# Linear attention and two feed-forward blocks on one core: VectorE's order written out for sixteen slots, the weight decode cut in other pieces

## The chip, the core and the metric

The kernel runs on one core of a Trainium2 chip. The metric is the device time of one execution in microseconds (us), the median of three runs. The engines are TensorE (PE: matmuls; PEld is its weight load), VectorE (DVE), ScalarE (ACT), GpSimd (POOL) and SyncE (SP, whose queue issues the transfers). They run side by side, each through its own list of instructions in order, and wait for each other through semaphores.

## The reference

Three stages follow each other. The first is a linear attention with a decaying state (batch 4, 8 heads, 768 steps, 48 wide), here as the recurrence that defines it:

```
cur   = (u * k_t) v_t^T
y_t   = r_t (state + cur)
state = w_t * state + k_t v_t^T
```

The second is a feed-forward block on the 3072 tokens that come out, 384 wide, with 2048 inner columns:

```
h = x @ w_in ;  g = h * clip(h + 3, 0, 6) / 6 ;  x = g @ w_out
```

The third is like it with 1024 inner columns, a softmax gate and a layer norm between its two products. The weights of both blocks come as float64, so their words have to be turned into float32 on the chip.

## The kernel before, in words

The attention works on tiles of 128 steps. One batch entry has six tiles, and tile number i is step block i // 4 of batch entry i % 4, so the state of a batch entry is needed again four tiles on. 512 tokens (four tiles) make a group of the first feed-forward block. A group takes 16 **slots**, one for each chunk of 128 inner columns; there are six groups and so 96 slots. Slot n issues `ffn_in(n)` (9 matmuls into h, L715, then ScalarE's t at L719, VectorE's gate at L720 and ScalarE's rounded copy gh at L721; GpSimd makes the rest gl at L729), then pieces of the attention of a later tile, then `ffn_out(n-2)` (9 matmuls, L740). Products are made three times, high by high, high by low and low by high part, so each operand has a high (`..h`) and a low (`..l`) half. The buffers `h` are two, so `ffn_in(n)` needs the gate of slot n-2 to be done.

In slots 0 to 15 a second stream runs along: the 16 chunks of the weights (`w1`) are decoded, chunk m needed by slot m. Chunks 0 to 2 are made ahead of the slots. Slot n then finishes chunk n+3 (`w1_b`), begins chunk n+4 (`w1_a`) and issues the load of chunk n+6 (`w1_load`, four transfers into one of three `raw` buffers). One chunk has 128x768 words in pairs, low word and high word of a float64:

- L63, ScalarE: absolute value of the high word times a power of two, into `dec`.
- L66, VectorE: the sign bit of the high word, in place in `raw`. It has to come after L63, which reads the same words.
- L50, VectorE: `dec` shifted left by 3, with the sign. L53, VectorE: the top 3 bits of the low word added. After L53 the `raw` buffer is free.
- L71, ScalarE: `w1_h`, the rounded copy. L72, VectorE: `w1_l`, what is left over.

The attention of tile 4+n//4 is spread over four slots; j is n % 4. Its VectorE work: in slot j=0 the masks' copies (L625, two of them, whose other operand ScalarE makes at L620); two state adds (L644), which need the products kv of TensorE (L635); in slot j=2 the output's low half xl (L686; its high half xh is ScalarE's L685). For the next tile then the scans over the decay, q (L525, four) and e (L529, L531 four, L535), and the product with the keys (L549), on which TensorE's transposes ktp (L578) wait. TensorE's small products share three buffers (`ps_a`) in turn, so rt (L489) waits until the state adds have read kv, and kt (L489) until xl has read yt.

What sets the order: through the whole loop only SP's list stands as written. The lists of the other engines come from the scheduler of the framework, which moved VectorE's instructions among the slots: the pieces of the decode of three chunks lie between those of the attention.

Of the kernel before, what the change touches and what calls it, by code (L numbers as in the profile page):

```python
# [8 lines left out]
F32 = mybir.dt.float32  # L9
BF16 = mybir.dt.bfloat16  # L10
F32R = mybir.dt.float32r
I32 = mybir.dt.int32
ACTF = mybir.ActivationFunctionType
ALU = mybir.AluOpType
# [4 lines left out]
P = 128  # L19
W_LO, W_HI = 0.75, 1.25  # L20
SIGN = -(2**31)
# [26 lines left out]
def dec_b(nc, raw, f):  # L48

    nc.vector.scalar_tensor_tensor(  # L50
        out=f, in0=f, scalar=3, in1=raw[:, :, 1], op0=ALU.logical_shift_left, op1=ALU.bitwise_or
    )
    nc.vector.scalar_tensor_tensor(  # L53
        out=f, in0=raw[:, :, 0], scalar=29, in1=f, op0=ALU.logical_shift_right, op1=ALU.bitwise_or
    )
    return f.bitcast(F32)


def dec_s(nc, pool, raw, total, bufs=2):

    f = pool.tile([P, raw.shape[1]], I32, tag="dec", name="dec", bufs=bufs)
    hw = raw[:, :, 1]
    nc.scalar.activation(  # L63
        out=f.bitcast(F32), in_=hw.bitcast(F32), func=ACTF.Abs, scale=2.0**-112, accum_out=total
    )
    nc.vector.tensor_scalar(out=hw, in0=hw, scalar1=SIGN, scalar2=None, op0=ALU.bitwise_and)  # L66
    return f


def split(nc, src, hi, lo, eng):  # L70
    nc.scalar.activation(out=hi, in_=src, func=ACTF.Copy)  # L71
    eng.tensor_tensor(out=lo, in0=src, in1=hi.bitcast(F32), op=ALU.subtract)  # L72
# [206 lines left out]
def fast_path(  # L279
# [14 lines left out]
    nc = tc.nc  # L294
    B, H, S, D = r.shape
# [8 lines left out]
    M1 = F1 // P  # L304
    M2 = F2 // P
    GT = B * C
    NTILE = NG * B
    NSLOT = NG * M1
    LAG = 2
    LATE = 10  # L310
    JOIN = 10
# [43 lines left out]
    w1_h = w1p.tile([P, M1, WN], F32R, name="w1_h")  # L355
# [16 lines left out]
        wst[m] = [t]  # L372

    def w1_a(m):
        wst[m].append(dec_s(nc, dec, wst[m][0], chk[:, 3 * NTILE + m:3 * NTILE + m + 1]))

    def w1_b(m):
        split(nc, dec_b(nc, *wst.pop(m)), w1_h[:, m, :], w1_l[:, m, :], nc.vector)


    s_st = []
# [127 lines left out]
        )  # L509

    def st0(i):
        a = at[i]
        g = i // B
        if i < LATE:
            wt = ps_in(i, "wt", "y0")
            trans(wt, a["w"])
            rt = ps_in(i, "rt", "y1")
            trans(rt, a["r"])
        else:
            wt, rt = flip("w"), flip("r")  # L520
        q = atp.tile([P, HP, C + 1], F32, tag="q", name="q")
        e = atp.tile([P, HP, C], F32, tag="e", name="e")
        nc.gpsimd.memset(q[0:DP, :, C:C + 1], 1.0)
        for hp in range(HP):
            nc.vector.tensor_tensor_scan(  # L525
                out=q[0:DP, hp, 0:C][:, ::-1], data0=wt[0:DP, hp, :][:, ::-1], data1=ones[0:DP, :],
                initial=1.0, op0=ALU.mult, op1=ALU.mult,
            )
        nc.vector.reciprocal(out=e[0:DP, :, 0], in_=q[0:DP, :, 0])  # L529
        for hp in range(HP):  # L530
            nc.vector.tensor_tensor_scan(  # L531
                out=e[0:DP, hp, 1:C], data0=wt[0:DP, hp, 0:C - 1], data1=ones[0:DP, 0:C - 1],
                initial=e[0:DP, hp, 0:1], op0=ALU.mult, op1=ALU.mult,
            )
        nc.vector.tensor_tensor(out=e[0:DP], in0=rt[0:DP], in1=e[0:DP], op=ALU.mult)  # L535
        a.update(q=q, e=e)

    def st1(i):
        a = at[i]
# [40 lines left out]
        nc.scalar.activation(out=ktok, in_=ktp[:, :, 0:DP], func=ACTF.Copy)  # L580
        a["ktok"] = ktok

    def scores(i):
        a = at[i]
        kq = a["q"][:, :, 1:C + 1]
        rr = a["e"]
        a["am"] = []
        pas = [ps_tile("pa0"), ps_tile("pa1")] if i < JOIN else late["pa"]
        d = atp.tile([P, H], F32, tag="d", name="d")
        nc.vector.tensor_reduce(out=d, in_=a["z"], axis=AX.X, op=ALU.add)  # L590
        if i < JOIN:
            mask, diag = (x.unsqueeze(1).to_broadcast([P, HP, C]) for x in (causal, ident))
            for j in range(HP):
                for hh, pa in enumerate(pas):
                    o = 64 * hh
                    nc.tensor.matmul(
                        out=pa[:, j, :], lhsT=kq[o:o + D, j, :], rhs=rr[o:o + D, j, :], start=True, stop=True
                    )
        else:
            mask, diag = late["mask"], late["diag"]  # L600
            d0 = d
            d = late["v"].tile([P, H], F32, tag="dt", name="dt")
            nc.gpsimd.tensor_copy(out=d[:, 0:4], in_=d0[:, 0:4])
            for o, n, t0 in turned:
                nc.gpsimd.tensor_copy(out=d[o:o + n, 4:8], in_=d0[t0:t0 + n, 4:8])
            for j in (0, 2, 1, 3):
                for ks in (0, 64):
                    for hh, pa in enumerate(pas):
                        o, p = 64 * hh, ks if j < 2 else 64 - ks
                        nc.tensor.matmul(  # L610
                            out=pa[p:p + 64, j, ks:C], lhsT=kq[o:o + D, j, ks:ks + 64], rhs=rr[o:o + D, j, ks:C],
                            start=True, stop=True, skip_group_check=True,
                        )
        dv = d.rearrange("p (j hh) -> p hh j", hh=2)
        for hh, pa in enumerate(pas):
            am = atp.tile([P, 4, C], F32, tag="am", name="am")
            a["am"].append(am)
            if i < JOIN:
                for j in range(HP):
                    nc.scalar.activation(out=am[:, j, :], in_=ident, func=ACTF.Copy, scale=dv[:, hh, j:j + 1])  # L620
            else:
                nc.gpsimd.tensor_tensor(
                    out=am, in0=diag, in1=dv[:, hh, :].unsqueeze(2).to_broadcast([P, HP, C]), op=ALU.mult,
                )
            nc.vector.copy_predicated(am, mask, pa)  # L625

    def state_add(i):
        a = at[i]
# [62 lines left out]
            scores(i)  # L691

    def st3(i):
        state_add(i)
        if JOIN <= i + 1 < NTILE:
            scores(i + 1)
        out_x(i)

    stages = [stw, st0, st1, st2, st3]


    g_t = {}
# [126 lines left out]
    def load_to(n):  # L829
        while nxt[0] < min(n, LATE):  # L830
            load_in(nxt[0])
            load_v(nxt[0])
            nxt[0] += 1

    LD = 3
# [10 lines left out]
    nxt[0] = 3  # L846
    starts = [0, 2, 3, 4]
    decodes = {4: [0, 1], 6: [2], 8: [3]}
    NS = len(stages)
    for tick in range(starts[-1] + NS):  # L850
        for i in range(B):
            s = tick - starts[i]
# [13 lines left out]
    for i in range(B, NTILE):  # L866
        for s in range(NS):
            back = 2 if s == NS - 1 else s - 3 if i < JOIN else s - 5
            sched.setdefault(4 * (i - B) + back, []).append((i, s))
    for n in sorted(q for q in sched if q < 0):  # L870
        for i, s in sched[n]:
            stages[s](i)
            if s == 3:
                load_to(i + 3)
    order = ctx.enter_context(ExitStack())
    order.enter_context(tc.manual_schedule(engines={mybir.EngineType.SP}))
    for n in range(NSLOT + LAG):
        if n < NSLOT:
            ffn_in(n)
        if n == 4 * (JOIN - B) - 2:  # L880
# [158 lines left out]
```

## Time and profile before

| | us |
|---|---|
| median of 3 runs | 769.21 (768.65 to 769.26) |
| the profiled execution, whole | 768.09 |
| its span in the trace | 766.3 |
| TensorE busy | 733.2 (96%) |
| VectorE busy | 530.8 (69%) |
| ScalarE busy | 355.6 (46%) |
| GpSimd busy | 225.7 (29%) |

The shares are means over the program. The change lies in slots 0 to 15, which are 104 us of it: slot 0 begins at 45.7 us and slot 16 at 149.5. What they say there has to be read from views of those stretches: the table by stretches (busy time of each engine, granted clock of TensorE, share of the DMA engines), the groups of instructions of one engine within a window, and the timeline of an engine, in which each row has its start, its duration and, in brackets, how long the engine had been idle ahead of it and what ended that. Rows that follow each other without a dependency overlap a little in the timeline, because an instruction's end is drawn after the next one's start.

### The profile page before, as it was taken

To read this page: it belongs to the slowest core of one execution; us is meant where nothing else is said; L and a number is where in the kernel's file an instruction comes from. 1 tells how busy PE (TensorE), PEld (TensorE's weight loads), DVE (VectorE), ACT (ScalarE), POOL (GpSimd) and SP (SyncE) were. 2 spreads that over 40 slices of the span, in tenths; PEclk is the share of its full clock that TensorE was granted. 3 is DMA by queue.
4 is the path that set the end of the run, shared out by engine and by line. 5 is a ranking of instruction groups with operands and counts; after the bars stand their busy time and mean duration, and the time that the engine had idled before them with its cause. 6 is when DMAs were issued, how large, how long until landed. Compare 5 with 4: busy or idle time off the path is not lost. (4 is left out here: it accounts for less than half of the span.)

```text
span 766.3 us, 14116 instructions
## 1 busy us (share of the span) xinstructions
PE 733.2 (96%) x5308; PEld 619.4 (81%) x5308; DVE 530.8 (69%) x1008; ACT 355.6 (46%) x727; POOL 225.7 (29%) x357
## 2 busy tenths in 40 slices
PE   7688997999999999999999999999999999999996
PEld 5456775888888888888888888888899999999995
DVE  6978898768777777777798845877655555555551
ACT  4675665643444443433334335554544444444442
POOL 5225426522322222233333311224322222222200
PEclk9798899999999999999999999999999999999999
DMA  9795763624444454435334204432211111111001
GB/s 164 177 168 137 178 140 93 127 69 98 96 94 95 120 108 96 97 107 117 70 75 113 53 1 125 125 103 62 73 42 42 42 52 42 42 42 42 32 21 36
DMA packets 151406, 67.31 MB, mean 88 GB/s; under 512 B 101793, under 2 KB 145953, under 8 KB 151329
## 3 DMA queue, kind: packets, MB, share of 16 engines
q1 hardware_dynamic: 151328, 66.32, 36.3%
q8 instruction: 44, 0.72, 0.4%
q14 instruction: 34, 0.27, 0.1%
HBM read 56.33 MB, written 9.44 MB: 86 GB/s over the span
## 5 line engine op out<-in xcount | busy, mean ns | idle before, releaser
L740 PE MATMUL y<-gh,w_h 128*128 128x512 f32 x288 | 116.1, 403 | 0.0
L715 PE MATMUL h<-xh,w_h 128*128 128x512 f32 x288 | 113.3, 394 | 0.7 <-ACT xh L685 0.7
L715 PE MATMUL h<-xl,w_h 128*128 128x512 f32 x288 | 113.3, 393 | 0.0
L740 PE MATMUL y<-gl,w_h 128*128 128x512 f32 x288 | 113.1, 393 | 0.0
L740 PE MATMUL y<-gh,w_l 128*128 128x512 f32 x288 | 113.0, 392 | 0.0
L715 PE MATMUL h<-xh,w_l 128*128 128x512 f32 x288 | 112.8, 392 | 0.0
L719 ACT ACTIVATE t<-h,cols 128x512 f32<-128x512 f32 x96 | 65.4, 682 | 87.4 <-PE h L715 87.2
L721 ACT ACTIVATE gh<-t 128x512 fp32r<-128x512 f32 x96 | 60.4, 629 | 96.5 <-DVE t L720 96.5
L720 DVE SCALAR_TENSOR_TENSOR t<-t,h 128x512 f32<-128x512 f32 x96 | 65.1, 679 | 38.1 <-ACT t L719 38.0
L729 DVE TENSOR_TENSOR gl<-t,gh 128x512 fp32r<-128x512 f32 x80 | 66.9, 836 | 21.1 <-ACT gh L721 19.0
L78 DVE TENSOR_REDUCE nm<-h 128x1 f32<-128x1024 f32 x24 | 29.4, 1224 | 61.5 <-PE h L946 61.5
L973 PE MATMUL po<-w_oh,qh 128*128 128x384 f32 x192 | 67.2, 350 | 0.3 <-ACT qh L962 0.3
L560 POOL TENSOR_TENSOR sp<-s_st,q 112x384 f32<-112x384 f32 x20 | 18.6, 931 | 163.1 <-PE yt L657 139.9
L740 PEld LDWEIGHTS y<-gh,w_h 128*128 128x128 f32 x288 | 54.4, 189 | 13.8 <-issue 2.8
L973 PE MATMUL po<-w_oh,ql 128*128 128x384 f32 x192 | 64.8, 337 | 0.1
L973 PE MATMUL po<-w_ol,qh 128*128 128x384 f32 x192 | 64.8, 338 | 0.0
L715 PEld LDWEIGHTS h<-xh,w_h 128*128 128x128 f32 x288 | 54.6, 190 | 12.5 <-ACT xh L685 0.9
L715 PEld LDWEIGHTS h<-xh,w_l 128*128 128x128 f32 x288 | 54.7, 190 | 11.5
L715 PEld LDWEIGHTS h<-xl,w_h 128*128 128x128 f32 x288 | 54.7, 190 | 11.4
L740 PEld LDWEIGHTS y<-gh,w_l 128*128 128x128 f32 x288 | 54.4, 189 | 11.6
L740 PEld LDWEIGHTS y<-gl,w_h 128*128 128x128 f32 x288 | 54.6, 190 | 10.2
L962 ACT ACTIVATE qh<-pt 128x512 fp32r<-128x512 f32 x48 | 26.1, 596 | 78.4 <-PE pt L960 78.4
(129 smaller groups left out, 1497.3 us busy)
## 6 DMA issues: line engine op xcount, KB each, us to landing
raw<-in_moe_w_out_dram SPq DMA_DIRECT2D x24, 384.0 KB, 6.0
raw<-in_moe_w_in_dram SPq DMA_DIRECT2D x48, 128.0 KB
r<-in_r_dram SPq DMA_DIRECT2D x24, 192.0 KB, 3.1
k<-in_k_dram SPq DMA_DIRECT2D x24, 192.0 KB, 3.7
y1d<-ye SPq DMA_DIRECT2D x18, 256.0 KB, 2.3
y<-y1d SPq DMA_DIRECT2D x24, 192.0 KB, 2.8
out_dram<-os SPq DMA_DIRECT2D x24, 192.0 KB, 1.9
v<-in_v_dram SPq DMA_DIRECT2D x20, 192.0 KB, 4.5
```

The source lines that it names most:

```text
L78: nc.vector.tensor_reduce(out=nm, in_=h, axis=AX.X, op=ALU.max, negate=True)
L560: nc.gpsimd.tensor_tensor(out=sp[0:DP], in0=s_st[b][0:DP], in1=q[0:DP, :, 0:1].to_broadcast([DP, HP, 2 * D]), op=ALU.mult)
L715: nc.tensor.matmul(out=h, lhsT=a, rhs=b, start=(j == 0), stop=(j == len(ops) - 1))
L719: nc.scalar.activation(out=t, in_=h, func=ACTF.Relu, bias=three)
L720: nc.vector.scalar_tensor_tensor(out=t, in0=t, scalar=6.0, in1=h, op0=ALU.min, op1=ALU.mult)
L721: nc.scalar.activation(out=gh, in_=t, func=ACTF.Copy)
L729: eng.tensor_tensor(out=gl, in0=t, in1=gh.bitcast(F32), op=ALU.subtract)
L740: nc.tensor.matmul(out=y_ps[g][c], lhsT=a, rhs=b, start=(m == 0 and j == 0), stop=(m == M1 - 1 and j == 2))
L962: nc.scalar.activation(out=qh[:, ms, :], in_=pt, func=ACTF.Copy)
L973: nc.tensor.matmul(out=po, lhsT=x[:, m, :], rhs=y[:, m, :], start=(n == 0), stop=(n == 3 * M2 - 1))
```

## The change

Slots 0 to 15 get a loop of their own, and in it VectorE's list too stands as written. Three things are in it.

The decode is cut otherwise. `dec_p` has ScalarE's absolute value as before, then two instructions of VectorE that write the low word's place instead of the high word's: the low word shifted right by 29 (L77 of the new kernel), then the sign bit of the high word joined to it (L78). Neither needs ScalarE's result. `dec_q` is one instruction (L84): `dec` shifted left by 3, joined with that word. The high copy is L403 (was L71) and the low half L407 (was L72). Four instructions of VectorE a chunk it was and is.

The written order of a slot: the merge (L84, L403) ahead of or behind `ffn_in`, the low half (L407) behind `ffn_out`, then L74, L77 and L78 of the next chunk. The copies of the masks (L669) are a step of their own, and the scans of the next tile are two steps: q in slot j=2, e and the product with the keys in slot j=3.

The state adds (L688, was L644) with TensorE's products kv and GpSimd's part of tiles 4 to 9 move from slot j=2 to slot j=1.

The lists of ScalarE, TensorE and GpSimd are still made by the scheduler, and change with it. SP's list is the same instruction for instruction.

```diff
--- before.py
+++ after.py
@@ -65,6 +65,26 @@
     )
     nc.vector.tensor_scalar(out=hw, in0=hw, scalar1=SIGN, scalar2=None, op0=ALU.bitwise_and)
     return f
+
+
+def dec_p(nc, pool, raw, total):
+
+    f = pool.tile([P, raw.shape[1]], I32, tag="dec", name="dec", bufs=2)
+    lw, hw = raw[:, :, 0], raw[:, :, 1]
+    nc.scalar.activation(
+        out=f.bitcast(F32), in_=hw.bitcast(F32), func=ACTF.Abs, scale=2.0**-112, accum_out=total
+    )
+    nc.vector.tensor_scalar(out=lw, in0=lw, scalar1=29, scalar2=None, op0=ALU.logical_shift_right)
+    nc.vector.scalar_tensor_tensor(out=lw, in0=hw, scalar=SIGN, in1=lw, op0=ALU.bitwise_and, op1=ALU.bitwise_or)
+    return f
+
+
+def dec_q(nc, raw, f):
+
+    nc.vector.scalar_tensor_tensor(
+        out=f, in0=f, scalar=3, in1=raw[:, :, 0], op0=ALU.logical_shift_left, op1=ALU.bitwise_or
+    )
+    return f.bitcast(F32)
 
 
 def split(nc, src, hi, lo, eng):
@@ -372,10 +392,21 @@
         wst[m] = [t]
 
     def w1_a(m):
-        wst[m].append(dec_s(nc, dec, wst[m][0], chk[:, 3 * NTILE + m:3 * NTILE + m + 1]))
+        wst[m].append(dec_p(nc, dec, wst[m][0], chk[:, 3 * NTILE + m:3 * NTILE + m + 1]))
 
     def w1_b(m):
-        split(nc, dec_b(nc, *wst.pop(m)), w1_h[:, m, :], w1_l[:, m, :], nc.vector)
+        w1_merge(m)
+        w1_low(m)
+
+    def w1_merge(m):
+        f = dec_q(nc, *wst.pop(m))
+        nc.scalar.activation(out=w1_h[:, m, :], in_=f, func=ACTF.Copy)
+        wst[m] = f
+
+    def w1_low(m):
+        nc.vector.tensor_tensor(
+            out=w1_l[:, m, :], in0=wst.pop(m), in1=w1_h[:, m, :].bitcast(F32), op=ALU.subtract
+        )
 
 
     s_st = []
@@ -509,6 +540,10 @@
         )
 
     def st0(i):
+        st0_q(i)
+        st0_e(i)
+
+    def st0_q(i):
         a = at[i]
         g = i // B
         if i < LATE:
@@ -526,6 +561,11 @@
                 out=q[0:DP, hp, 0:C][:, ::-1], data0=wt[0:DP, hp, :][:, ::-1], data1=ones[0:DP, :],
                 initial=1.0, op0=ALU.mult, op1=ALU.mult,
             )
+        a.update(q=q, e=e, wt=wt, rt=rt)
+
+    def st0_e(i):
+        a = at[i]
+        q, e, wt, rt = a["q"], a["e"], a.pop("wt"), a.pop("rt")
         nc.vector.reciprocal(out=e[0:DP, :, 0], in_=q[0:DP, :, 0])
         for hp in range(HP):
             nc.vector.tensor_tensor_scan(
@@ -533,7 +573,6 @@
                 initial=e[0:DP, hp, 0:1], op0=ALU.mult, op1=ALU.mult,
             )
         nc.vector.tensor_tensor(out=e[0:DP], in0=rt[0:DP], in1=e[0:DP], op=ALU.mult)
-        a.update(q=q, e=e)
 
     def st1(i):
         a = at[i]
@@ -580,11 +619,11 @@
         nc.scalar.activation(out=ktok, in_=ktp[:, :, 0:DP], func=ACTF.Copy)
         a["ktok"] = ktok
 
-    def scores(i):
+    def scores(i, later=False):
         a = at[i]
         kq = a["q"][:, :, 1:C + 1]
         rr = a["e"]
-        a["am"] = []
+        a["am"], a["masks"] = [], []
         pas = [ps_tile("pa0"), ps_tile("pa1")] if i < JOIN else late["pa"]
         d = atp.tile([P, H], F32, tag="d", name="d")
         nc.vector.tensor_reduce(out=d, in_=a["z"], axis=AX.X, op=ALU.add)
@@ -622,7 +661,12 @@
                 nc.gpsimd.tensor_tensor(
                     out=am, in0=diag, in1=dv[:, hh, :].unsqueeze(2).to_broadcast([P, HP, C]), op=ALU.mult,
                 )
-            nc.vector.copy_predicated(am, mask, pa)
+            a["masks"].append((am, mask, pa))
+            if not later:
+                am_copy(i)
+
+    def am_copy(i):
+        nc.vector.copy_predicated(*at[i]["masks"].pop(0))
 
     def state_add(i):
         a = at[i]
@@ -691,12 +735,13 @@
             scores(i)
 
     def st3(i):
-        state_add(i)
+        if not B <= i < JOIN:
+            state_add(i)
         if JOIN <= i + 1 < NTILE:
             scores(i + 1)
         out_x(i)
 
-    stages = [stw, st0, st1, st2, st3]
+    stages = [stw, st0, st1, st2, st3, state_add]
 
 
     g_t = {}
@@ -846,7 +891,7 @@
     nxt[0] = 3
     starts = [0, 2, 3, 4]
     decodes = {4: [0, 1], 6: [2], 8: [3]}
-    NS = len(stages)
+    NS = len(stages) - 1
     for tick in range(starts[-1] + NS):
         for i in range(B):
             s = tick - starts[i]
@@ -867,14 +912,55 @@
         for s in range(NS):
             back = 2 if s == NS - 1 else s - 3 if i < JOIN else s - 5
             sched.setdefault(4 * (i - B) + back, []).append((i, s))
+        if i < JOIN:
+            sched.setdefault(4 * (i - B) + 1, []).append((i, NS))
     for n in sorted(q for q in sched if q < 0):
         for i, s in sched[n]:
             stages[s](i)
             if s == 3:
                 load_to(i + 3)
     order = ctx.enter_context(ExitStack())
+    order.enter_context(tc.manual_schedule(engines={mybir.EngineType.SP, mybir.EngineType.DVE}))
+    for n in range(M1):
+        j, ti = n % 4, B + n // 4
+        if j == 0:
+            w1_merge(n + LD) if n + LD < M1 else None
+            keys_in(ti)
+            scores(ti, later=True)
+            ffn_in(n)
+        elif j == 1:
+            am_copy(ti)
+            w1_merge(n + LD) if n + LD < M1 else None
+            state_add(ti)
+            ffn_in(n)
+            stw(ti + 1)
+        elif j == 2:
+            w1_merge(n + LD) if n + LD < M1 else None
+            ffn_in(n)
+            out_x(ti)
+        else:
+            st0_e(ti + 1)
+            ffn_in(n)
+            w1_merge(n + LD) if n + LD < M1 else None
+            st1(ti + 1)
+        if j == 0:
+            load_to(ti + 3)
+        if n >= LAG:
+            ffn_out(n - LAG)
+        if n + LD < M1:
+            w1_low(n + LD)
+        if n + LD + 1 < M1:
+            w1_a(n + LD + 1)
+        if n + LD + 3 < M1:
+            w1_load(n + LD + 3)
+        if j == 0:
+            am_copy(ti)
+        if j == 2:
+            st0_q(ti + 1)
+    order.close()
+    order = ctx.enter_context(ExitStack())
     order.enter_context(tc.manual_schedule(engines={mybir.EngineType.SP}))
-    for n in range(NSLOT + LAG):
+    for n in range(M1, NSLOT + LAG):
         if n < NSLOT:
             ffn_in(n)
         if n == 4 * (JOIN - B) - 2:
```

VectorE's list in slots 5 and 6, before (dec_1000, dec_1041 are the chunks 8 and 9, raw_1003 the words of chunk 10; t is the gate, xl the output's low half, q and e the scans of the next tile):

```order
L720 SCALAR_TENSOR_TENSOR t_1059<-t_1059,h_1049 128x512
L644 TENSOR_TENSOR s_st1_115<-kv_1066,sp_900 48x4x48
L72 TENSOR_TENSOR w1_l_112<-dec_1000,w1_h_111 128x768
L644 TENSOR_TENSOR s_st1_115<-kv_1066,sp_900 48x4x48
L686 TENSOR_TENSOR xl_828<-yt_1077,xh_827 128x3x128
L525 SCALAR_TENSOR_TENSOR q_1118<-wt_1108,ones_91 112x128 x4
L50 SCALAR_TENSOR_TENSOR dec_1041<-dec_1041,raw_923 128x768
L529 RECIPROCAL e_1119<-q_1118 112x4
L66 TENSOR_SCALAR raw_1003<-raw_1003 128x768
L531 SCALAR_TENSOR_TENSOR e_1119<-wt_1108,e_1119,ones_91 112x127 x4
L53 SCALAR_TENSOR_TENSOR dec_1041<-raw_923,dec_1041 128x768
L535 TENSOR_TENSOR e_1119<-rt_1113,e_1119 112x512
```

The same place in the new kernel (dec_1052 is chunk 9, raw_1002 the words of chunk 10):

```order
L688 TENSOR_TENSOR s_st1_115<-kv_1011,sp_903 48x4x48 x2
L765 SCALAR_TENSOR_TENSOR t_1032<-t_1032,h_1022 128x512
L407 TENSOR_TENSOR w1_l_112<-dec_998,w1_h_111 128x768
L77 TENSOR_SCALAR raw_924<-raw_924 128x768
L78 SCALAR_TENSOR_TENSOR raw_924<-raw_924 128x768
L84 SCALAR_TENSOR_TENSOR dec_1052<-dec_1052,raw_924 128x768
L765 SCALAR_TENSOR_TENSOR t_1073<-t_1073,h_1063 128x512
L730 TENSOR_TENSOR xl_831<-yt_1080,xh_830 128x3x128
L407 TENSOR_TENSOR w1_l_112<-dec_1052,w1_h_111 128x768
L77 TENSOR_SCALAR raw_1002<-raw_1002 128x768
L78 SCALAR_TENSOR_TENSOR raw_1002<-raw_1002 128x768
L560 SCALAR_TENSOR_TENSOR q_1140<-wt_1130,ones_91 112x128 x4
```

The low half of chunk 9 now stands ahead of the scans, where the one before stood behind all of them, and each chunk's four pieces stand together.

ScalarE's list in the same slots, before (dec_1144 is chunk 10):

```order
L507 ACTIVATE junk_1299,chk_71<-w_976,cols_66 128x384
L71 ACTIVATE w1_h_111<-dec_1000 128x768
L721 ACTIVATE gh_1060<-t_1059 128x512
L685 ACTIVATE xh_827,chk_71<-yt_1077 128x3x128
L63 ACTIVATE dec_1144,chk_71<-raw_1003 128x768
L719 ACTIVATE t_1162<-h_1152,cols_66 128x512
L71 ACTIVATE w1_h_111<-dec_1041 128x768
```

And in the new kernel (dec_1121 is chunk 10):

```order
L764 ACTIVATE t_1073<-h_1063,cols_66 128x512
L535 ACTIVATE junk_1313,chk_71<-w_977,cols_66 128x384
L403 ACTIVATE w1_h_111<-dec_998 128x768
L766 ACTIVATE gh_1033<-t_1032 128x512
L729 ACTIVATE xh_830,chk_71<-yt_1080 128x3x128
L538 ACTIVATE junk_1313,chk_71<-w_977,cols_66 128x384
L74 ACTIVATE dec_1121,chk_71<-raw_1002 128x768
L403 ACTIVATE w1_h_111<-dec_1052 128x768
```

The absolute value of chunk 10 still stands ahead of the high copy of chunk 9, on which VectorE's low half of chunk 9 waits; the junk activations, which sum an input tile, now stand around the high copy of chunk 8.

## Rows read from the trace of the kernel before

**Rows 1.** The page: busy time, share and instructions of each engine.

```profile
PE 733.2 (96%) x5308; PEld 619.4 (81%) x5308; DVE 530.8 (69%) x1008; ACT 355.6 (46%) x727; POOL 225.7 (29%) x357
```

**Rows 2.** Slots: window, length, engines' busy, PEclk, DMA share, GB/s.

```profile
52.90:69.30 16.40, 13.86 (x123) 11.23 (x122) 10.83 (x20) 8.74 (x18) 8.21 (x8) 0.90 0.67 168
69.30:98.10 28.80, 25.11 (x178) 20.01 (x177) 26.01 (x43) 16.96 (x38) 12.81 (x15) 0.88 0.59 151
98.10:126.40 28.30, 23.72 (x177) 18.89 (x176) 25.70 (x40) 16.34 (x35) 11.17 (x12) 0.94 0.65 150
126.40:149.50 23.10, 21.88 (x177) 17.85 (x176) 18.05 (x31) 16.55 (x40) 12.22 (x16) 1.00 0.43 84
149.50:171.20 21.70, 21.70 (x177) 17.94 (x177) 13.32 (x27) 10.38 (x23) 7.08 (x11) 1.00 0.33 83
```

**Rows 3.** VectorE's groups, 46 to 150 us: busy, mean | idle before.

```profile
L50 DVE SCALAR_TENSOR_TENSOR dec<-dec,raw 128x768 int32<-128x768 int32 x13 | 16.6, 1275 | 0.0
L72 DVE TENSOR_TENSOR w_l<-dec,w_h 128x768 fp32r<-128x768 f32 x13 | 12.4, 957 | 2.5 <-ACT w_h L71 2.3
L53 DVE SCALAR_TENSOR_TENSOR dec<-raw,dec 128x768 int32<-128x768 int32 x13 | 12.3, 945 | 0.0
L720 DVE SCALAR_TENSOR_TENSOR t<-t,h 128x512 f32<-128x512 f32 x16 | 10.9, 680 | 0.7 <-ACT t L719 0.6
...
L66 DVE TENSOR_SCALAR raw<-raw 128x768 int32<-128x768 int32 x12 | 7.3, 610 | 10.1 <-ACT dec L63 7.0 <-DMA w<-in_w_dram 3.1
```

**Rows 4.** VectorE's timeline, L66 alone: start, duration, [idle ahead, releaser].

```profile
61.00 0.56 DVE L66 TENSOR_SCALAR raw<-raw 128x768 int32<-128x768 int32 x1 [0.48 <-ACT dec L63]
...
69.53 0.92 DVE L66 TENSOR_SCALAR raw<-raw 128x768 int32<-128x768 int32 x1 [2.20 <-ACT dec L63]
...
88.67 0.58 DVE L66 TENSOR_SCALAR raw<-raw 128x768 int32<-128x768 int32 x1 [1.67 <-ACT dec L63]
...
95.95 0.56 DVE L66 TENSOR_SCALAR raw<-raw 128x768 int32<-128x768 int32 x1 [0.67 <-ACT dec L63]
...
114.63 0.56 DVE L66 TENSOR_SCALAR raw<-raw 128x768 int32<-128x768 int32 x1 [1.56 <-ACT dec L63]
...
121.74 0.81 DVE L66 TENSOR_SCALAR raw<-raw 128x768 int32<-128x768 int32 x1 [0.41 <-ACT dec L63]
```

**Rows 5.** ScalarE's timeline, slots 6 to 10.

```profile
87.01 0.62 ACT L504 ACTIVATE junk<-w,cols 128x384 bf16<-128x384 f32 x1 [1.98 <-DMA w<-in_w_dram]
...
94.91 0.92 ACT L63 ACTIVATE dec<-raw 128x768 f32<-128x768 f32 x1 [2.85 <-DMA raw<-in_moe_w_out_dram]
...
98.90 0.85 ACT L71 ACTIVATE w_h<-dec 128x768 fp32r<-128x768 f32 x1 [2.38 <-DVE dec L53]
...
120.69 0.93 ACT L63 ACTIVATE dec<-raw 128x768 f32<-128x768 f32 x1 [2.54 <-DMA raw<-in_moe_w_out_dram]
```

**Rows 6.** VectorE's timeline, slot 15, where nothing waits in between.

```profile
146.01 0.56 DVE L590 TENSOR_REDUCE d<-r 128x8 f32<-128x384 f32 x1 [1.48 <-POOL r L552]
146.49 0.17 DVE L529 RECIPROCAL e<-q 112x4 f32<-112x4 f32 x1
146.69 1.60 DVE L531 TENSOR_TENSOR_SCAN e<-wt,e,ones 112x127 f32<-112x127 f32 x4
148.40 0.69 DVE L535 TENSOR_TENSOR e<-rt,e 112x512 f32<-112x512 f32 x1
```

**Rows 7.** VectorE's timeline, slots 10 to 12.

```profile
118.56 0.56 DVE L686 TENSOR_TENSOR xl<-yt,xh 128x384 fp32r<-128x384 f32 x1
119.03 1.36 DVE L525 TENSOR_TENSOR_SCAN q<-wt,ones 112x128 f32<-112x128 f32 x4
...
129.10 0.68 DVE L549 TENSOR_TENSOR q<-kt,q 112x512 f32<-112x512 f32 x1
```

**Rows 8.** TensorE's timeline, slot 10.

```profile
118.63 0.62 PE L489 MATMUL rt<-ident,r 128*112 128x128 f32 x4 [3.73 <-issue]
```

**Rows 9.** SyncE's timeline, slots 6 and 7.

```profile
88.94 0.45 SPq L371 DMA_DIRECT2D raw<-in_moe_w_out_dram  x1
```

## The prediction

> **What bounds the kernel now.** Over the whole span TensorE is the bound: 96% busy against VectorE's 69% [rows 1]. That mean hides the stage that is changed, so I read the table by stretches next, cut at the starts of slots 2, 4, 8, 12, 16 and 20 [rows 2]. The last stretch, behind the decode, shows what TensorE needs alone for four slots: 21.7 us, all of it busy, at full granted clock (1.00). Slots 4 to 8 take 28.8 and slots 8 to 12 take 28.3, with a granted clock of 0.88 and 0.94, so TensorE ran a part of them at the lower of its two levels after it had stood idle. VectorE is busy for 26.0 and 25.7 of them. So in slots 4 to 12 VectorE is the bound, with 2.8 and 2.6 us idle; in slots 2 and 3 it is idle for 5.6 of 16.4. Slots 12 to 16, with VectorE 18.1 busy of 23.1, are close to TensorE's 21.7 already. The ceiling of any gain is then 28.8 + 28.3 + 23.1 - 3 x 21.7 = 15.1 us in slots 4 to 16, and what slots 2 and 3 hold.
>
> What VectorE waits for I read from its groups in 46 to 150 us [rows 3]. Nearly all of the idle time stands ahead of L66: 10.1 us before 12 instructions. A small part, 2.5, stands ahead of the low half L72. The timeline of those L66 [rows 4] beside ScalarE's [rows 5] shows two kinds of wait. In slots 6 and 10 ScalarE's L63 itself had waited for the raw words to land (94.91, 120.69) and L66 starts 1.04 and 1.05 us after it: the words were the last to come. The waits at 88.67 and 114.63 are others: there ScalarE had stood for an input tile's w (1.98 us idle ahead of the junk row at 87.01) with L63 queued behind it.
>
> **The work of VectorE** is the same in number: before, a chunk takes L66, L50, L53 and L72; after, L77, L78, L84 and L407. L78, L84 and L407 have the forms of L53, L50 and L72, with the same tile sizes (L50 without GpSimd beside it is near L53: 0.95 [rows 3]; its mean of 1.28 has rows that GpSimd's use of the same memory stretches). L77 is the one new form, a shift with a number. Its nearest row is L66, a bitwise instruction of the same shape on the same words, at 0.56 undisturbed [rows 4]; the other end is L53, which has a shift in it and two inputs, at 0.95 [rows 3]. I take 0.56, since L66 has one input as L77 has, so this term is 0, with +0.39 x 12 = +4.7 as its other end; nothing lets it be cheaper than L66. The Trainium skill ("VectorE: DVE Perf Modes", section "The perf-mode tier table (the rule you actually need)") has a float32 tensor_scalar in SBUF run at twice the rate of two-input forms; whether an integer shift keeps that no row here shows.
>
> **What goes: the waits ahead of L66.** L77 and L78 need only the words in place, which is when L63 starts. Where the words are last to come, each wait shrinks by the 1.03 to 1.05 by which L66 lags L63, but by no more than the wait: 0.67 at 95.95, 0.41 at 121.74. I take the ones in slots 2 to 4 to be of that kind too: 0.48 at 61.00, 1.03 at 69.53, and 1.03 of the seventh wait (10.1 less the six shown [rows 4], 3.1). Together 3.6. The two behind the junk rows go whole: 1.67 + 1.56 = 3.2. Sum **-6.8 us**. The second ends are 0 (VectorE then waits for something else) and -10.1.
>
> **What comes: pauses between dependent instructions.** In slot 15, L529 starts 0.08 us before the row ahead of it, on which it doesn't depend, has ended (146.49 against 146.01 + 0.56), while L531, which reads L529's result, starts 0.03 after that one's end (146.69 against 146.66) [rows 6]. A dependency on the instruction just ahead thus costs 0.11. Before, the scheduler had put other work between the pieces of a chunk. Now L78 follows L77 at once in 12 chunks, and L84 follows L78 at once in 6: 18 x 0.11 = **+2.0**. The other end is 0. The Trainium skill (same page, section "The DRAIN you can't avoid") says that the semaphore between two consecutive instructions "costs nothing extra here"; by that the sum would be 2.0 lower. The rows at 146.49 and 146.69 disagree, and the measurement decides.
>
> **What comes: the low half waits in order.** L407 needs ScalarE's high copy L403, and in slots 6 and 10 (and 2) ScalarE's list has the absolute value of the next chunk, which waits for its words, ahead of that copy. It is so before too, but there L72 stands behind all scans of the next tile, so VectorE had work. Now L407 stands ahead of L77, L78 and the scans. VectorE goes on only after landing + absolute value 1.02 + copy 0.85 [rows 5], that is 1.9 after the landing, where the sum above had let it go on at the landing itself. The bounds are 0 (the words come earlier, or VectorE is late itself) and 1.9 a group. I take 1.5, near the upper end, since the words were last in both groups shown; 3 x 1.5 = **+4.5**. In slots j=3, L84, L588 and L407 follow each other: the copy of 0.85 begins when L84 ends and L588 covers 0.60 of it (0.68 less the overlap of 0.08); with the pause some 0.35 stay, 3 x 0.35 = **+1.0** (0 to 1.5). The 2.5 that L72 waits already [rows 3] I leave as they are: in slots j=1 L403 stands behind a junk row and the next slot's t on ScalarE, much as before.
>
> A walk through slots 10 and 11 puts a second figure beside that. The words land at 120.69; L407 of that chunk starts at 120.69 + 1.02 + 0.85 = 122.6. Behind it come L407 itself 0.95, L77 0.56, L78 0.95, the four q scans 1.36, the reciprocal 0.17, the e scans 1.60, their product 0.69, the gate 0.68 and L84 0.95 [rows 3, 6, 7], together 7.9, less eight overlaps of 0.08 and with four or five pauses of 0.11: L588 starts at 130.4. Before, L549 started at 129.10. So the keys' product, on which TensorE's ktp waits, comes 1.3 us later, though a chunk and a half of decode is further along behind it, which the next group gets back in part.
>
> **What is moved: the state products.** TensorE's rt stands 3.73 us idle at 118.63 [rows 8], since its buffer is freed by the second state add, which stood behind the gate of slot 10 and a low half. With the adds one slot sooner this goes. I give it 0: VectorE bounds those slots, and the same list then makes kt wait for xl and ktp for the product above. Its ends are 0 and -3.7 in each of two groups, inside the ceiling and not on top of -6.8. SP's list is the same, so no transfer is moved past another; loads move only as their `raw` buffers come free.
>
> **After slot 16** the scheduler's lists for tiles 8 and 9 differ too: a gate L765 of 0.68 [rows 3] stands ahead of the product with the keys. TensorE has no gap there (21.70 of 21.70 [rows 2]), so what it waits is lost: 0 to 2 x 0.68, I take **+1.0**, since nothing else lies in its list to cover it.
>
> **Sum:** -6.8 + 2.0 + 4.5 + 1.0 + 1.0 = +1.7 us on the profiled execution's 768.09 (span 766.3 and 1.8 around it), that is 769.8. That execution stands 1.12 below the median of 769.21, to which I add the same difference: **770.9**.
>
> **The rivals.** A measurement of this kernel can tell about 0.2% from no change, 1.5 us: faster is under 767.7, slower over 770.7.
>
> A, the forecast: the waits for ScalarE's absolute value become waits for its high copy. Its own range is 768.9 (the last two terms 0) to 773.0 (the last three at their upper ends, +1.2, +0.5 and +0.4). It would show as idle time ahead of L407 in slots 2, 6 and 10.
>
> B, the waits go and none comes in their place. If the words land sooner, because L84 in one instruction frees `raw` sooner and nothing of the old order holds VectorE, the terms +4.5, +1.0 and +1.0 are 0, and -6.8 + 2.0 = -4.8 stay: **764.4**. For it: VectorE is the bound there and 10.1 of its idle time is aimed at; TensorE would also stand at the higher level of its clock for longer. Against: L63 was waiting for the words in both groups shown [rows 5], and only their landing releases it.
>
> C, the shift doesn't run as L66 does. With 0.95 each instead of 0.56, +4.7 on VectorE where it is the bound: **775.6**. It decides from slot 4 on, in each chunk. For it: integer two-input forms take 0.95. Against: L66 is an integer form too.
>
> D, nothing moves, because the transfers set the pace. The words that come last in a group land at 94.91 and 120.69 [rows 5], 25.8 apart, nearly a group's length. The first of these are issued at 88.94 [rows 9] and are there 6.0 later, behind an input tile's loads, and SP's list is unchanged. Then the end of slot 12 stays where it is: **769.2**. Against: VectorE's 26 us busy explain the same length.
>
> **How the numbers follow.** A 0.42, B 0.24, C 0.17, D 0.17. Of A's own range some four tenths lie below 770.7, so A gives 0.16 to no change and 0.26 to slower. Faster: B and a little of the low side of A, 0.25. Same: D's 0.17 and A's 0.16, 0.33. Slower: C and the rest of A, 0.42. The range goes from B's 764.4 to C's 775.6, which leaves half of each of these out, 2 in 10.
>
> **What would show it.** In the profile after: no idle time ahead of L78 and little ahead of L77 (the first term); L77 at 0.56 (against C); idle time ahead of L407, released by L403, of 4 us or more in 46 to 150 (A; under 2 speaks for B); L63's successor L74 starting at nearly the same times as L63 (D) or sooner (B); rt without its 3.73; and slot 16 within 2 us of 149.5, with the rest of the difference after it. Wrong would be the forecast if L77 took over 0.8, or if TensorE's granted clock rose to 1.00 in slots 4 to 12.

## The result, and the profile after

The changed kernel takes 774.17 us (median of 5 runs, 772.80 to 775.21) against 769.21 (5 runs, 768.13 to 770.28). The ratio is 1.007 with a 95% interval of 1.0057 to 1.0082: 5.0 us slower. The forecast was 770.9, within 764.4 to 775.6. The profiled execution took 774.17 as well, with a span of 772.5, so it stands 6.1 above the profiled execution before.

The table by stretches of the new kernel, cut at the starts of the same slots (4, 8, 12, 16 and 20) as [rows 2], the first stretch from 52.9 to slot 4:

```profile
52.90:74.70 21.80, 15.90 (x138) 12.47 (x137) 16.89 (x19) 12.10 (x29) 7.77 (x8) 0.87 0.70 174
74.70:102.77 28.07, 24.54 (x177) 19.09 (x176) 27.34 (x39) 16.64 (x36) 10.17 (x12) 0.93 0.54 136
102.77:129.05 26.28, 23.80 (x177) 18.47 (x176) 24.98 (x37) 16.14 (x35) 10.64 (x12) 0.95 0.61 143
129.05:153.60 24.55, 22.90 (x177) 18.26 (x176) 19.71 (x39) 13.31 (x31) 10.68 (x18) 0.97 0.37 68
153.60:176.14 22.54, 22.19 (x177) 17.77 (x176) 14.78 (x30) 12.77 (x32) 7.19 (x11) 1.00 0.41 94
```

Slot 16 begins at 153.60 and began at 149.50, 4.1 later. The cuts at slots 4, 8 and 12 compare less well, since the scheduler put TensorE's small products at other places among the slots; slot 16, behind the decode, is a safe mark. From there the new kernel loses another 2.0: 0.8 up to slot 20 (22.54 against 21.70) and 1.2 between slots 21 and 23. VectorE is busy nearly all the time from slot 4 to 12: for 27.34 of 28.07 and for 24.98 of 26.28. Most of the idle time is gone, and busy time took its place.

VectorE's groups in the same window as [rows 3] (46 us to slot 16 and a little beyond):

```profile
L84 DVE SCALAR_TENSOR_TENSOR dec<-dec,raw 128x768 int32<-128x768 int32 x13 | 16.4, 1261 | 0.2
L78 DVE SCALAR_TENSOR_TENSOR raw<-raw 128x768 int32<-128x768 int32 x13 | 15.1, 1163 | 0.4
L407 DVE TENSOR_TENSOR w_l<-dec,w_h 128x768 fp32r<-128x768 f32 x13 | 12.8, 981 | 3.3 <-ACT w_h L403 3.3
...
L77 DVE TENSOR_SCALAR raw<-raw 128x768 int32<-128x768 int32 x12 | 11.6, 964 | 1.9 <-DMA raw<-in_moe_w_out_dram 1.9
```

The 10.1 us of idle time ahead of L66 have become 1.9 ahead of L77, as meant. The low half waits for 3.3, hardly more than the 2.5 before. But the four groups are busy for 55.9 us, and the old four for 48.6, though their number and their undisturbed durations are the same. The timeline of VectorE in slots 4 to 6 shows where that comes from (start, duration, idle ahead and releaser):

```profile
81.36 1.07 DVE L407 TENSOR_TENSOR w_l<-dec,w_h 128x768 fp32r<-128x768 f32 x1 [0.31 <-ACT w_h L403]
82.35 0.56 DVE L77 TENSOR_SCALAR raw<-raw 128x768 int32<-128x768 int32 x1
82.94 0.96 DVE L78 SCALAR_TENSOR_TENSOR raw<-raw 128x768 int32<-128x768 int32 x1
...
92.99 1.79 DVE L77 TENSOR_SCALAR raw<-raw 128x768 int32<-128x768 int32 x1
94.82 1.66 DVE L78 SCALAR_TENSOR_TENSOR raw<-raw 128x768 int32<-128x768 int32 x1
96.51 1.65 DVE L84 SCALAR_TENSOR_TENSOR dec<-dec,raw 128x768 int32<-128x768 int32 x1
...
99.16 0.94 DVE L407 TENSOR_TENSOR w_l<-dec,w_h 128x768 fp32r<-128x768 f32 x1
100.02 1.78 DVE L77 TENSOR_SCALAR raw<-raw 128x768 int32<-128x768 int32 x1
```

And GpSimd's timeline beside it, in the same columns:

```profile
92.94 1.29 POOL L774 TENSOR_TENSOR gl<-t,gh 128x512 fp32r<-128x512 f32 x1 [2.92 <-ACT gh L766]
...
94.32 1.34 POOL L590 TENSOR_TENSOR r<-r,k 128x384 f32<-128x384 f32 x1
95.74 1.61 POOL L591 TENSOR_TENSOR r<-r,u_bc 128x384 f32<-128x384 f32 x1
99.64 1.59 POOL L774 TENSOR_TENSOR gl<-t,gh 128x512 fp32r<-128x512 f32 x1 [2.29 <-ACT gh L766]
```

At 82.35 L77 takes 0.56. At 100.02 it begins while GpSimd's gl runs from 99.64 to 101.23, and it ends at 101.80, which is 0.57 after gl: it stood until gl had ended and then took its usual time. The row at 92.99 (gl to 94.23, L77 to 94.78) is the same. The Trainium skill ("SBUF — State Buffer", section "SBUF: two separate sides") says that VectorE and GpSimd have one pair of ports in common, for which an instruction of VectorE competes when it runs in a 2-port mode or has two inputs in SBUF; the first of the two engines keeps the pair for its whole instruction while the other "fully blocks". These rows agree with it. For the forecast I had taken each piece at its undisturbed time.

TensorE's waits in 46 to 200 us, grouped by what it waited for (total, times, longest); the kernel before, its two largest:

```profile
PE rt L489 <- issue: 5.3, 3, 3.7
PE ktp L578 <- DVE q L549: 4.8, 3, 2.7
```

and the changed kernel, its three largest:

```profile
PE kt L520 <- DVE xl L730: 8.3, 3, 3.4
PE yt L701 <- DVE am L669: 2.8, 2, 2.3
PE h L760 <- DVE t L765: 2.2, 2, 1.6
```

The wait of rt is gone, and kt, which follows it on the same three buffers, waits for VectorE's xl instead.

### The profile page after: what moved, and what is told of

Read it like the earlier page. It is cut to its first block, busy times and chain, and to the rows that moved or that the text cites. A ratio compares the mean times of both kernels' runs of the same rounds, so it can differ in the third digit from the quotient of the medians.

```text
span 772.5 us, 14117 instructions
## 1 busy us (share of the span) xinstructions
PE 737.3 (95%) x5308; PEld 620.2 (80%) x5308; DVE 540.2 (70%) x1008; ACT 356.3 (46%) x727; POOL 221.0 (29%) x357
```

## The experiments

Three theories stood at the start. P: the decode pieces, in a row behind the gate, collide with GpSimd. Q: the written order lets something stand late, either xl (Q1) or the low half, which waits for ScalarE's high copy (Q2). R: the new pieces are dearer in themselves. All times are medians beside runs of the kernel before on the same chip; in brackets the ratio to these and its interval.

**The new decode alone,** in the scheduler's order:

```diff
 def w1_a(m):
-    wst[m].append(dec_s(nc, dec, wst[m][0], ...))
+    wst[m].append(dec_p(nc, dec, wst[m][0], ...))
 def w1_b(m):
-    split(nc, dec_b(nc, *wst.pop(m)), ...)
+    split(nc, dec_q(nc, *wst.pop(m)), ...)
```

> The kernel before with the new decode alone (absolute value, L77 and L78 of the low word's place, one merge); order of VectorE and the state adds as the scheduler makes them. Theory P (the new written order puts three decode pieces in a row where GpSimd works, and each waits for GpSimd's use of the memory they share): the pieces stay spread, their four groups are stretched by about 5 us as before and not 12, the waits ahead of L66 (10.1) shrink to 2 to 4; the time is 763 to 767. Theory Q (the order makes new waits, xl and the low half standing late): the same, 763 to 767. Theory R (the new pieces are themselves dearer, by their pauses and their shift): 771 to 775.

767.35 us against 768.80 (0.9978, 0.9967 to 0.9989): 1.5 faster. R falls, and the time lies just above the 763 to 767 that both P and Q expected. VectorE's groups of that kernel (L92 is the low half):

```profile
L92 DVE TENSOR_TENSOR w_l<-dec,w_h 128x768 fp32r<-128x768 f32 x13 | 14.7, 1129 | 1.3 <-ACT w_h L91 1.2
L78 DVE SCALAR_TENSOR_TENSOR raw<-raw 128x768 int32<-128x768 int32 x13 | 14.4, 1112 | 0.0
L84 DVE SCALAR_TENSOR_TENSOR dec<-dec,raw 128x768 int32<-128x768 int32 x13 | 13.6, 1044 | 0.0
...
L77 DVE TENSOR_SCALAR raw<-raw 128x768 int32<-128x768 int32 x12 | 8.9, 741 | 5.6 <-DMA raw<-in_moe_w_out_dram 5.6
```

The waits fall from 10.1 + 2.5 to 5.6 + 1.3, 5.7 less, and the busy time rises from 48.6 to 51.6. So 2.7 were left to gain, and 1.5 came.

**The old decode in the written order,** state products sooner as in the change:

```diff
-    wst[m].append(dec_p(nc, dec, wst[m][0], ...))
+    wst[m].append(dec_s(nc, dec, wst[m][0], ...))
-    f = dec_q(nc, *wst.pop(m))
+    f = dec_b(nc, *wst.pop(m))
```

> The changed kernel with the old decode (sign bit by L66 behind ScalarE's absolute value, two merges) in the same written order, state adds one slot sooner. P: the pieces L66, L50, L53 stand where L77, L78, L84 did and are stretched as much (groups together 10 us or more over their undisturbed times), and waits ahead of L66 come back on top: 776 to 782. Q: the waits of the order stay and L66's come back: 776 to 782 too, but the stretch is near the 5 us of before. R: under 771.

778.05 us (1.0121, 1.0098 to 1.0145), in the range that P and Q both gave. So the written order with the sooner state products costs 9.2 with the old decode. Its pieces L66, L50 and L53 are busy for 48.1 where they were busy for 36.2 [rows 3]:

```profile
L50 DVE SCALAR_TENSOR_TENSOR dec<-dec,raw 128x768 int32<-128x768 int32 x13 | 18.0, 1381 | 0.2
L53 DVE SCALAR_TENSOR_TENSOR dec<-raw,dec 128x768 int32<-128x768 int32 x13 | 17.5, 1344 | 0.4
L66 DVE TENSOR_SCALAR raw<-raw 128x768 int32<-128x768 int32 x12 | 12.6, 1054 | 2.7 <-ACT dec L63 2.7
```

The order stretches the pieces whichever decode is used, as P has it. Of the waits only 2.7 came back, not the 10.

**GpSimd's gl left out** in slots 3 to 15, in the kernel before and in the changed one (the products read slot 2's low part there, which leaves out that part of the sum):

```diff
+    gl2 = []
 ...
-        gl = ffp.tile([P, GT], F32R, tag="gl", name="gl")
+        gl = gl2[0] if 3 <= n < M1 else ffp.tile([P, GT], F32R, tag="gl", name="gl")
+        gl2[:] = [gl]
 ...
-        if n <= NA:
+        if n <= NA and not 3 <= n < M1:
             ffn_low(n)
```

> The kernel before without GpSimd's low part gl in slots 3 to 15 (the products there read slot 2's). P: the 4.8 us by which L50 and L66 are stretched shrink to under 2 and the time falls by 2 to 5, to 764 to 767. Q: within 1 of 769.

768.49 us (0.9994, 0.9982 to 1.0007): the time that Q expected. The stretch of L50 and L66 does shrink as P has it, from 4.8 to 1.3 us, but no time comes of it, and L66 waits for 11.5 where it waited for 10.1:

```profile
L50 DVE SCALAR_TENSOR_TENSOR dec<-dec,raw 128x768 int32<-128x768 int32 x13 | 12.7, 974 | 0.0
...
L66 DVE TENSOR_SCALAR raw<-raw 128x768 int32<-128x768 int32 x12 | 7.7, 643 | 11.5 <-ACT dec L63 11.4
```

> The changed kernel without GpSimd's low part gl in slots 3 to 15 (the products there read slot 2's). P: the 12 us of stretch shrink to 3 to 5, the time falls by 5 to 9, to 765 to 769, and stands within 2 of the kernel before without gl. Q: it falls by less than 3 and stays 4 to 5 above the kernel before without gl.

772.89 us (1.0057, 1.0040 to 1.0075). The two stand 4.4 apart, nearly as far as with gl, as Q has it. P falls in the form in which I had put it. Two groups of the changed kernel without gl:

```profile
L407 DVE TENSOR_TENSOR w_l<-dec,w_h 128x768 fp32r<-128x768 f32 x13 | 12.4, 957 | 10.2 <-ACT w_h L403 10.2
...
L77 DVE TENSOR_SCALAR raw<-raw 128x768 int32<-128x768 int32 x12 | 7.9, 659 | 1.5 <-DMA raw<-in_moe_w_out_dram 1.5
```

L77 shrinks from 11.6 to 7.9 us, all four groups from 55.9 to 49.3, and the low half waits for 10.2 where it waited for 3.3. The collisions had covered a wait that the order makes: VectorE arrives at the low half late, so it does not wait, or it arrives in time and waits for the high copy.

**The tile's output xl sooner,** ahead of three decode pieces:

```diff
             ffn_in(n)
             stw(ti + 1)
+            out_x(ti)
 ...
             ffn_in(n)
-            out_x(ti)
```

> The changed kernel with the tile's output (yt, xh, xl) issued in slot j=1 behind the state adds, so that xl stands ahead of three decode pieces. Theory Q1 (xl stands too late in the written order, and TensorE's kt waits for its buffer: 8.3 us): the wait of kt goes and the time falls by 2 to 4, to 770 to 772. Theory Q2 (low halves wait in order for ScalarE's high copy, and VectorE is late by that whatever else stands where): TensorE's wait moves on to ktp or h and the time stays within 1 of 774.

780.42 us (1.0151, 1.0128 to 1.0173): 6 us slower than the change. The wait of kt does go, but TensorE then waits for VectorE's gate, and the low half waits for the high copy in nine places. One row of TensorE's waits and one of VectorE's:

```profile
PE h L760 <- DVE t L765: 13.4, 7, 3.8
```

```profile
DVE w_l L407 <- ACT w_h L403: 8.8, 9, 3.3
```

Neither expectation has this time. Q1 falls as it was put: with kt's wait for xl gone, the largest of TensorE's in the changed kernel, the time rose. But the edit makes new waits too, so this run alone does not show what kt's wait cost.

**The state adds back** in slot j=2:

```diff
-            state_add(ti)
             ffn_in(n)
             stw(ti + 1)
 ...
             ffn_in(n)
+            state_add(ti)
             out_x(ti)
```

> The changed kernel with the state products and adds in slot j=2, where they were before. If the earlier place costs something (the adds wait for kv ahead of the decode): under 772.5. If it gains something: 776 or more, with TensorE's waits for rt back at 3 us or more. If it does nothing, as the forecast has it: within 1.5 of 774.

776.22 us (1.0097, 1.0081 to 1.0114), 2 slower than the change, with rt waiting again, as the second of the expected outcomes has it:

```profile
PE h L760 <- DVE t L765: 9.0, 6, 4.2
PE rt L520 <- issue: 6.8, 3, 3.5
```

Within the written order, the sooner adds gain 2.

**Each low half one slot later,** at the head of the next slot:

```diff
         j, ti = n % 4, B + n // 4
+        if 1 <= n <= M1 - LD:
+            w1_low(n + LD - 1)
 ...
-        if n + LD < M1:
-            w1_low(n + LD)
```

> The changed kernel with each low half L407 one slot later, at the head of the next slot, when its high copy is long made. Q2: the idle time ahead of L407 (3.3 us) goes, absolute values need not be waited for in slots j=1 and j=2, and the time falls by 2 to 5, to 769 to 772. Q1: kt's wait for xl stays near 8, and the time within 1.5 of 774.

767.98 us (0.9991, 0.9979 to 1.0003). That gives back 6.2, all that the change had lost and a little more than the 2 to 5 that Q2 expected. No low half waits any more. Q2 stands; its time was put too high.

**Both edits,** xl sooner and the low halves later:

> Both edits: the output in slot j=1 and the low halves one slot later. If Q1 and Q2 together are the cost of the written order: 765 to 769, level with the new decode in the scheduler's order (767.35) or under it. If the cost is elsewhere (the collisions with GpSimd, 12 us of stretch): 771 or more.

772.70 us (1.0049, 1.0033 to 1.0066). That is over the 765 to 769 of the first expectation and in the range of the second, but it does not show the collisions as the cost: with the low halves later, xl in slot j=1 costs 4.7. Now VectorE waits for ScalarE's xh there, and TensorE for the gate behind it:

```profile
DVE xl L730 <- ACT xh L729: 4.3, 3, 2.4
```

**The low half later in slots j=2 alone** (slots 2, 6 and 10), where the forecast had put its price:

```diff
         j, ti = n % 4, B + n // 4
+        if j == 3 and n <= M1 - LD:
+            w1_low(n + LD - 1)
 ...
-        if n + LD < M1:
+        if n + LD < M1 and j != 2:
             w1_low(n + LD)
```

> The changed kernel with the low half one slot later in the slots j=2 alone (slots 2, 6 and 10), where the forecast put +4.5 of the price. If the price is there: 769.5 to 771, that is most of the 6.2 that all low halves later gave back (774.17 to 767.98). If it is spread over all slots, or in j=1, where the high copy stands behind the next slot's t and a junk row: 772.5 to 774.

768.73 us (0.9997, 0.9985 to 1.0009): 5.4 of the 6.2 lie in these three places, a little more than expected. VectorE's timeline of this kernel in slot 6, the place of 98.69 to 102 above:

```profile
95.10 0.55 DVE L730 TENSOR_TENSOR xl<-yt,xh 128x384 fp32r<-128x384 f32 x1
95.57 0.55 DVE L77 TENSOR_SCALAR raw<-raw 128x768 int32<-128x768 int32 x1
96.15 0.96 DVE L78 SCALAR_TENSOR_TENSOR raw<-raw 128x768 int32<-128x768 int32 x1
97.03 1.36 DVE L560 TENSOR_TENSOR_SCAN q<-wt,ones 112x128 f32<-112x128 f32 x4
98.31 0.93 DVE L407 TENSOR_TENSOR w_l<-dec,w_h 128x768 fp32r<-128x768 f32 x1
```

and GpSimd's gl there:

```profile
96.18 2.07 POOL L774 TENSOR_TENSOR gl<-t,gh 128x512 fp32r<-128x512 f32 x1 [2.42 <-ACT gh L766]
```

L77 now runs ahead of gl at 0.55, and it is gl that waits (2.07 against 1.29). In the changed kernel the low half had pushed L77 into gl in each of the three slots: 1.78, 1.78 and 1.79 where 0.55 is usual, 3.7 together. With the waits of the low half there, 1.51 at 71.41, none at 99.16 and 0.59 at 126.58, that is 5.8, near the 5.4 that the runs give. The rows of the changed kernel in slots 2 and 10:

```profile
71.41 0.96 DVE L407 TENSOR_TENSOR w_l<-dec,w_h 128x768 fp32r<-128x768 f32 x1 [1.51 <-ACT w_h L403]
72.28 1.78 DVE L77 TENSOR_SCALAR raw<-raw 128x768 int32<-128x768 int32 x1
...
126.58 0.96 DVE L407 TENSOR_TENSOR w_l<-dec,w_h 128x768 fp32r<-128x768 f32 x1 [0.59 <-ACT w_h L403]
127.46 1.79 DVE L77 TENSOR_SCALAR raw<-raw 128x768 int32<-128x768 int32 x1
```

So it is the low half of one chunk and the next chunk's L77 that stand together in these slots. TensorE's kt waits for xl no less than in the changed kernel (8.3 there), and the time came back all the same:

```profile
PE kt L520 <- DVE xl L730: 8.9, 3, 3.6
```

This settles Q1: kt's wait was not what cost the 5.4.

**The new decode with the sooner state products,** in the scheduler's order:

```diff
     def st3(i):
-        state_add(i)
+        if not B <= i < JOIN:
+            state_add(i)
 ...
+        if i < JOIN:
+            sched.setdefault(4 * (i - B) + 1, []).append((i, NS))
```

> The kernel before with two of the change's parts, the new decode and the state products one slot sooner, and with the scheduler's order for VectorE. If the earlier state products gain by themselves (TensorE's waits for rt, 7.9 us with the new decode alone, go): 764 to 766.5. If VectorE's order decides and they are worth nothing, as the forecast has it: within 1 of the 767.35 of the new decode alone. If they cost: over 768.5.

771.63 us against 769.18 (1.0040, 1.0025 to 1.0056). In the scheduler's order the sooner state products turn a gain of 1.5 into a loss of 2.4. TensorE's waits for rt go, and others come in their place:

```profile
PE ktp L598 <- DVE q L569: 6.4, 3, 2.9
PE kt L509 <- DVE xl L706: 3.3, 2, 3.2
```

**VectorE's list written through slot 23,** with the low halves later:

```diff
-    order.enter_context(tc.manual_schedule(engines={mybir.EngineType.SP}))
+    order.enter_context(tc.manual_schedule(engines={mybir.EngineType.SP, mybir.EngineType.DVE}))
     for n in range(M1, NSLOT + LAG):
+        if n == 24:
+            ...
```

> The changed kernel with the low halves one slot later, and with VectorE's list as written through slot 23 and not 15. If what is lost behind slot 16 (0.9 us in that kernel, 0.7 to 1.2 in the changed one) comes from the scheduler's list there: slots 19 to 21 take what they took before (12.2 us) and the time is 766.5 to 767.5 against 768. If the written list waits there too (gl directly behind each gate): 768 to 771.

771.83 us (1.0042, 1.0026 to 1.0057), 3.9 slower and just over the second range. The stretch meant is slots 21 to 23 (the numbers in the expectation are two too low): 177.04 to 189.24 before, 12.2 us, and 19.2 in this kernel. The code's order is worse there than the scheduler's. That the scheduler's new list loses time behind slot 16 is read from the traces; this run does not mend it and so does not test it.

**The low halves later, and gl left out** as above:

> The changed kernel with the low halves one slot later and without GpSimd's low part gl in slots 3 to 15 (the products there read slot 2's). If the collisions with GpSimd cost once VectorE no longer waits for the high copies (some 8 us of stretch in the decode pieces there): 762 to 766. If they lie in time in which something else is late anyway (the landing of the words, ScalarE): within 1 of 768.

769.92 us (1.0010, 0.9998 to 1.0021), 1.9 over the run with gl and outside both expectations, though the two intervals overlap. Taking gl away gains nothing here either, though hardly a piece is stretched any more: the four groups are busy for 44.5 us, with gl for 50.7. VectorE waits for the words to land instead:

```profile
DVE raw L77 <- DMA raw<-in_moe_w_out_dram: 8.1, 4, 2.2
```

## Why the prediction was right, and where it was off

The direction was right, and so was the place that decides, the low half in slots j=2. The size was not: +1.7 was forecast and 5.0 measured (6.1 between the two profiled executions). That the time lies in the stated range is luck. It is above A's own range, which ended at 773.0, and inside only because the stated range reached to C's 775.6; C's mechanism, a dearer shift, is not what happened. Nor did the signs come as put. Slot 16 begins 4.1 later and not within 2; the low half waits for 3.3, between the 4 of A and the 2 of B; L77 takes 0.96 in the mean, over the 0.8 at which the forecast called itself wrong, though 0.55 to 0.56 undisturbed; and L74 starts 2.3 and 4.1 after the times of L63 (97.22 and 124.82 against 94.91 and 120.69), which no rival had. Kept were the little idle time ahead of L77 and L78 (1.9 and 0.4), rt without its wait, and a granted clock under 1.00 in slots 4 to 12. Step by step:

- *VectorE bounds slots 4 to 12.* Right by its busy share, 27.34 of 28.07 after, but that share holds time in which VectorE stands for GpSimd. Without gl its pieces are busy for 6.6 us less in the changed kernel, and L50 and L66 for 3.5 less in the kernel before; the time fell by 1.3 and 0.3, neither clear of the noise. So a microsecond of VectorE is not one of time there, as the sum took it.
- *The waits ahead of L66 go, -6.8.* The waits went, and more of them: 10.1 to 1.9. As a gain it was oversized. With the new decode alone the waits of pieces and low half fell by 5.7, 3.0 came back as longer pieces, and 1.5 of time was gained. The step took each wait removed for time gained, because VectorE was the bound. (The seventh wait, 3.1, was ended by an input tile's w [rows 3], not by words, as the step had it.)
- *The work of VectorE is the same, 0 (with +4.7 as other end).* This is the term that failed. The shift costs what L66 cost (0.55 to 0.56), so rival C is out. But the pieces are busy for 7.3 us more, nearly all of it because they now stand where GpSimd works. Taking gl away gave back only 1.3 of time, since the wait for the high copy then comes out (10.2): the two are not added, the one covers the other.
- *The low half waits in order, +4.5 in slots j=2.* The place is shown by the run with the low half later in these slots alone (5.4 back). The price was near, but it is made otherwise: 2.1 of waiting and 3.7 of L77 pushed into gl. Without gl the waiting in slots 2, 6 and 10 is 3.7 (1.15, 1.83 and 0.70), of 10.2 in all.
- *+1.0 in slots j=3.* Right in size: the row at 81.36 has 0.31 where 0.35 was put, and it is 0.31 too at 109.09 and 137.36.
- *The pauses, +2.0.* The rows agree: L78 at 82.94 starts 0.03 after L77's end (82.35 + 0.56), where L77 started 0.08 ahead of the end of the row before it. No run takes them away alone.
- *The state products, 0.* Not 0 in either order: +4.3 in the scheduler's (771.63 against 767.35) and -2.0 in the written one (774.17 against 776.22).
- *Behind slot 16, +1.0.* It is 2.0 in the profile. The mechanism was another for 1.2 of it: in slot 22 TensorE's h waits for a gate that stands behind the scans of e, not a ktp behind a gate. This wait is 0.59; the rest of the 1.2 is TensorE's busy time (12.77 against 12.06 for the same stretch) and its cause open. VectorE's rows, then TensorE's:

```profile
185.72 1.59 DVE L571 TENSOR_TENSOR_SCAN e<-wt,e,ones 112x127 f32<-112x127 f32 x4
187.22 0.66 DVE L765 SCALAR_TENSOR_TENSOR t<-t,h 128x512 f32<-128x512 f32 x1
```

```profile
187.94 0.50 PE L760 MATMUL h<-xh,w_h 128*128 128x512 f32 x1 [0.59 <-DVE t L765]
```

- *Rival D,* the landing of the words as the pace: not the pace of the changed kernel. The words of slot 6 come at 97.22 there, 2.3 later than the 94.91 of before [rows 5]. In the run with the low halves later and without gl it shows as the next wait.

Two things stay open. Without the term of slots j=2 the forecast's sum is -2.8, and the run that takes this term away stands at -0.5 (interval -1.2 to +0.7). The collisions in slots j=1, 1.79, 1.66 and 1.65 at 92.99 to 96.51, are in that run too, and GpSimd's products of r stand behind two of the three. They are hardly the missing 2.3 by themselves: in the run with all low halves later and without gl they are all but gone, and the time did not fall. What the 2.3 are is not shown. And the 2.0 behind slot 16 belong to the scheduler's list, which no run mended: the kernel with the low half later in slots j=2 begins slot 16 at 147.74, 1.8 ahead of the kernel before, and ends level with it.

The fastest kernel of the study is the new decode alone, in the scheduler's order: 767.35, 0.2% under the kernel before.

## What to carry to other kernels

A wait taken off the busiest engine of a stage is worth what remains after the next thing in its list: look what stands behind it, and what another engine does at that time. When an order is written by hand, try a step that needs a copy made by another engine a round later, behind work that needs nothing: here that was worth 5.4 us in three places. And the largest of TensorE's waits need not be the one that costs time: kt's wait for xl stayed, and those 5.4 us came back. Busy time in a trace can be standing time: compare an instruction's mean with its shortest rows before you call its engine the bound.

## What the runs showed of the hardware

That a decode piece of VectorE, with its words in SBUF, stands still while a product of GpSimd runs was in the trace of before, in L50's mean of 1275 ns against 950. I had read it as a detail of L50. It holds for each of the integer pieces: L77 0.55 or 1.79, L78 0.96 or 1.93, L84 0.95 or 2.03. The gate (680 ns in the mean, before and after), which reads h from PSUM, is not stretched: at 124.84 it takes 0.67 in the changed kernel, while GpSimd's L591 runs from 124.18 to 125.79. The delay goes both ways: gl takes 1.29 alone and 2.07 where L78 has begun just ahead of it.
